# Experts of a sparse-attention + MoE kernel: the last seven token tiles computed inside a branch on a count of used tiles

## The chip, the core and the metric

The kernel runs on one core of one Trainium2 chip. The metric is the device time of one execution in microseconds; lower is better. A core has five engines that run their own instruction streams and meet only at semaphores: TensorE (PE, matrix multiplies, with its weight loads shown as PEld), VectorE (DVE), ScalarE (ACT), GpSimd (POOL) and SyncE (SP, which here only issues transfers). A name with a q behind it (POOLq, PEldq) stands for the sequencer of that engine: the part that reads instructions, waits at semaphores, loads registers and takes branches.

## The reference

Eight batches of 576 tokens go through eight heads of attention of width 64 (four heads with a local window of 32, four with a stride of 32). The result, laid out as 4608 rows of 512 numbers, goes through a mixture of experts with one expert for each token:

```python
logits = np.einsum('bsd,de->bse', x, w_gate)
local_gate = 1.0 / (1.0 + np.exp(-np.einsum('bsd,de->bse', x, w_local).squeeze(-1)))
for b in range(B):
    prev_e = -1
    for s in range(S):
        fresh_e = int(np.argmax(logits[b, s]))
        if s == 0 or local_gate[b, s] < 0.5:
            e = fresh_e
        else:
            e = prev_e if prev_e >= 0 else fresh_e
        prev_e = e
        ...
        h = np.maximum(x[b, s] @ w1[e], 0.0)
        out[b, s] = p[e] * (h @ w2[e])
```

w1 of one expert is 512 x 1024 and w2 is 1024 x 512, all in f32. So each expert takes the rows that were routed to it, and the number of rows differs from expert to expert. With the inputs of the reference (fixed seed) the eight experts get 701, 469, 606, 495, 656, 452, 546 and 683 rows.

## The kernel before

**Attention** (0 to about 190 us) writes the 4608 rows `x` to a buffer `xd` in device memory and keeps gate probabilities and expert codes on chip. **Routing** (`route`, to about 243 us) counts the rows of each expert, rounds each count up to tiles of 128 rows (`nti`, `nt`), and gives each row a slot in a list of tiles in which expert follows expert. The list has a fixed length of `NT = (4608 + 8*127)//128 = 43` tiles, which is enough for every possible routing. Routing leaves four tables: `et` (the expert of each of the 43 tiles), `gi` and `si` (for each slot the row to read and the row to write) and `ps_slot` (its probability). A slot that no token holds reads row 0 and has a row number behind the end of `out`, so its write is dropped.

**Experts** (`experts`, from about 243 us to the end) goes through the 43 tiles, numbered j = 0 to 42 here. Each tile has five steps:

- `load(j)`: SP reads the tile's expert number from `et` into a register and issues the transfers of w1 and w2 of that expert, 2 MB each, into one of four buffers (`wp`, bufs=4); POOL gathers the 128 rows of `xd` into `xg` (`xp`, bufs=3) with an indirect transfer.
- `turn_x(j)`: four PE transposes into `xps`, then DVE copies them to `xgT`.
- `hidden(j)`: 2 x 4 x 4 products of 128x128 with w1 (64 PE rows in the profile, since an f32 product is done in two passes); ACT does the two ReLUs.
- `output(j)`: eight products of 128x512 with w2 (16 rows); ACT scales the result by `ps_slot` into `y`.
- at the end of `output(j)` POOL scatters `y` to `out` with an indirect transfer.

The program is written with a framework that traces these Python loops, orders the instructions of each engine by a scheduler of its own and puts in all semaphore waits. A buffer is reused only when its last reader has signalled: the gather of `xg` for tile j+3 waits until PE has transposed tile j, and the transfers of w1 and w2 for tile j+4 wait until PE has done `hidden(j)` and `output(j)`. Each engine works through its own list strictly in order.

Around all this stands one branch that exists already: `passes` is run once, then a count `bad` is loaded into a register of every engine (L98), and a second, careful pass is run only when it is above zero (L100). It is not run with these inputs. On the way that is not taken, each engine adjusts the semaphores that the skipped instructions would have raised; on POOL this is an instruction named INC_SWDGE_SEM, which adds to the eight semaphores of POOL's transfers.

Of the kernel before, what the change touches and what calls it, by code (L numbers as in the profile page):

```python
# [8 lines left out]
F32 = mybir.dt.float32  # L9
BF16 = mybir.dt.bfloat16  # L10
I32 = mybir.dt.int32
Act = mybir.ActivationFunctionType
Alu = mybir.AluOpType
# [5 lines left out]
P = 128  # L19
B, H, S, DH = 8, 8, 576, 64  # L20
D = H * DH
E, F = 8, 1024
DK, FK = D // P, F // P
N = B * S
# [16 lines left out]


NT = (N + E * (P - 1)) // P
SKIP = 8192
NEG = -8.0e9

# [36 lines left out]
@with_exitstack  # L83
def attention_then_scomoe(ctx: ExitStack, tc: tile.TileContext, q, k, vl, vs, wg, w1, w2, out):


    nc = tc.nc
    once = ctx.enter_context(tc.tile_pool(name="once", bufs=1))
    dram = ctx.enter_context(tc.tile_pool(name="dram", bufs=1, space=DRAM))
    xd = dram.tile([N, D], F32, name="xd")  # L90
    ident = once.tile([P, P], F32, name="ident")
    make_identity(nc, ident)
    sums = once.tile([P, B * PAIRS * 2, 2, 3], F32, name="sums")
    nc.gpsimd.memset(sums, 1.0)
    bad = once.tile([1, 1], I32, name="bad")

    passes(tc, False, q, k, vl, vs, wg, w1, w2, out, xd, ident, sums, bad)
    again = nc.values_load(bad[0:1, 0:1], min_val=0, max_val=P,  # L98
                           skip_runtime_bounds_check_because="a count of partitions")
    with tc.If(again > 0):  # L100
        passes(tc, True, q, k, vl, vs, wg, w1, w2, out, xd, ident, sums, bad)


def passes(tc, careful, q, k, vl, vs, wg, w1, w2, out, xd, ident, sums, bad):
    with ExitStack() as ctx:
        slots = ctx.enter_context(tc.tile_pool(name="slots", bufs=1))
        gi = slots.tile([P, NT], I32, name="gi")
        si = slots.tile([P, NT], I32, name="si")
        ps_slot = slots.tile([P, NT], F32, name="ps_slot")
        et = slots.tile([1, NT], I32, name="et")  # L110
        with ExitStack() as first:
            routing = first.enter_context(tc.tile_pool(name="routing", bufs=1))
            probs = routing.tile([LQ, LT, B, E], F32, name="probs")
            codes = routing.tile([LQ, LT, B, E], F32, name="codes")
            with ExitStack() as part:
                attention(part, tc, careful, q, k, vl, vs, wg, xd, ident, probs, codes, sums)
            with ExitStack() as part:
                route(part, tc, ident, probs, codes, gi, si, ps_slot, et)
            if not careful:
                with ExitStack() as part:  # L120
                    bounds(part, tc, sums, bad)
        with ExitStack() as part:
            experts(part, tc, xd, w1, w2, out, ident, gi, si, ps_slot, et)


def bounds(ctx, tc, sums, bad):

    nc = tc.nc
    bp = ctx.enter_context(tc.tile_pool(name="bp", bufs=1))
    bps = ctx.enter_context(tc.tile_pool(name="bps", bufs=1, space=PSUM))  # L130
    flat = sums.rearrange("p u h i -> p (u h i)")
    ok = bp.tile([P, B * PAIRS * 12], F32, name="ok")
    nc.vector.tensor_scalar(ok, flat, SUM_LO, None, Alu.is_ge)
    nc.vector.scalar_tensor_tensor(ok, flat, SUM_HI, ok, Alu.is_le, Alu.mult)
    low = bp.tile([P, 1], F32, name="low")
    nc.vector.tensor_reduce(low, ok, axis=AX.X, op=Alu.min)
    one = bp.tile([P, 1], F32, name="one")
    nc.vector.memset(one, 1.0)
    ps = bps.tile([1, 1], F32, name="bps")
    nc.tensor.matmul(ps, lhsT=low, rhs=one, start=True, stop=True)  # L140
    nc.vector.tensor_scalar(bad, ps, -1.0, float(P), Alu.mult, Alu.add)
# [254 lines left out]
def route(ctx, tc, ident, probs, codes, gi, si, ps_slot, et):  # L396

    nc = tc.nc
    rp = ctx.enter_context(tc.tile_pool(name="rp", bufs=1))
    pp = ctx.enter_context(tc.tile_pool(name="rps", bufs=1, space=PSUM))  # L400
# [32 lines left out]
    ones = rp.tile([R, S], F32, name="ones")  # L433
# [6 lines left out]
    for t in range(LT):  # L440
        nc.tensor.matmul(cps[:, t // 3, (t % 3) * LQ:(t % 3 + 1) * LQ],
                         lhsT=codes[:, t].rearrange("p b e -> p (b e)"), rhs=ident[0:LQ, 0:LQ],
                         start=True, stop=True)
# [21 lines left out]
    nt = rp.tile([R, 1], F32, name="nt")  # L465
# [5 lines left out]
    nc.vector.tensor_tensor(end, nn[0:E, 2:3], nt[0:E], op=Alu.add)  # L471
    over = rp.tile([E, NT], F32, name="over")
    nc.vector.tensor_scalar(over, io[0:E, 0:NT], end, None, Alu.is_ge)
    eps = pp.tile([1, NT], F32, name="eps")
    nc.tensor.matmul(eps, lhsT=ones[0:E, 0:1], rhs=over, start=True, stop=True)
    nc.vector.tensor_scalar(et, eps, float(E - 1), None, Alu.min)
    base = rp.tile([R, 1], F32, name="base")
    nc.vector.tensor_scalar(base, nn[:, 2:3], float(P), nn[:, 1:2], Alu.mult, Alu.add)
    nc.vector.tensor_scalar(base, base, -1.0, None, Alu.add)
# [37 lines left out]
    skip = rp.tile([P, NT], F32, name="skip")  # L517
    nc.vector.tensor_scalar(skip, tab[:, 0], 0.0, float(SKIP), Alu.is_equal, Alu.mult)
    nc.vector.tensor_tensor(row, row, skip, op=Alu.add)
# [3 lines left out]
def experts(ctx, tc, xd, w1, w2, out, ident, gi, si, ps_slot, et):  # L523


    nc = tc.nc
    wp = ctx.enter_context(tc.tile_pool(name="wp", bufs=4))
    xp = ctx.enter_context(tc.tile_pool(name="xp", bufs=3))
    psx = ctx.enter_context(tc.tile_pool(name="psx", bufs=2, space=PSUM))
    psh = ctx.enter_context(tc.tile_pool(name="psh", bufs=4, space=PSUM))  # L530
    psy = ctx.enter_context(tc.tile_pool(name="psy", bufs=2, space=PSUM))
    T = [dict() for _ in range(NT)]
    HB = 4

    def load(j):
        t = T[j]
        e = nc.values_load(et[0:1, j:j + 1], engines=[ET.SP], min_val=0, max_val=E - 1,
                           skip_runtime_bounds_check_because="a count of at most 8 experts, held to 7")
        t["w1"] = wp.tile([P, DK, F], F32, name="w1t")
        nc.sync.dma_start(out=t["w1"], in_=w1[bass.ds(e, 1)].rearrange("o (k p) f -> p (o k) f", p=P))  # L540
        t["w2"] = wp.tile([P, FK, D], F32, name="w2t")
        nc.sync.dma_start(out=t["w2"], in_=w2[bass.ds(e, 1)].rearrange("o (k p) f -> p (o k) f", p=P))
        t["x"] = xp.tile([P, D], F32, name="xg")
        nc.gpsimd.indirect_dma_start(out=t["x"], out_offset=None, in_=xd,  # L544
                                     in_offset=bass.IndirectOffsetOnAxis(ap=gi[:, j:j + 1], axis=0))

    def turn_x(j):
        t = T[j]
        ps = psx.tile([P, D], F32, name="xps")
        for kk in range(DK):  # L550
            nc.tensor.transpose(ps[:, kk * P:(kk + 1) * P], t["x"][:, kk * P:(kk + 1) * P], ident)  # L551
        t["xT"] = xp.tile([P, D], F32, name="xgT")
        nc.vector.tensor_copy(t["xT"], ps)  # L553

    def hidden(j):
        t = T[j]
        t["hT"] = xp.tile([P, FK, P], F32, name="hT", bufs=2)
        for g in range(FK // HB):
            ps = psh.tile([P, HB, P], F32, name="hps")
            for i in range(HB):  # L560
                c = slice((g * HB + i) * P, (g * HB + i + 1) * P)
                for kk in range(DK):
                    nc.tensor.matmul(ps[:, i], lhsT=t["w1"][:, kk, c], rhs=t["xT"][:, kk * P:(kk + 1) * P],  # L563
                                     start=(kk == 0), stop=(kk == DK - 1))
            nc.scalar.activation(t["hT"][:, g * HB:(g + 1) * HB], ps, Act.Relu)  # L565

    def output(j):
        t = T[j]
        ps = psy.tile([P, D], F32, name="yps")
        for kk in range(FK):  # L570
            nc.tensor.matmul(ps, lhsT=t["hT"][:, kk], rhs=t["w2"][:, kk, :],  # L571
                             start=(kk == 0), stop=(kk == FK - 1))
        y = xp.tile([P, D], F32, name="y")
        nc.scalar.activation(y, ps, Act.Copy, scale=ps_slot[:, j:j + 1])  # L574
        nc.gpsimd.indirect_dma_start(out=out, out_offset=bass.IndirectOffsetOnAxis(ap=si[:, j:j + 1], axis=0),  # L575
                                     in_=y, in_offset=None, bounds_check=N - 1, oob_is_err=False)

    load(0)
    load(1)
    turn_x(0)  # L580
    for j in range(NT):
        if j + 2 < NT:
            load(j + 2)
        hidden(j)
        if j + 1 < NT:
            turn_x(j + 1)
        output(j)


def _strided(a):  # L590
# [45 lines left out]
```

## Time and profile before

| what | us |
|---|---|
| median of 3 runs (lowest to highest) | 891.71 (890.55 to 892.64) |
| the profiled execution: time | 892.51 |
| the profiled execution: span from first to last instruction | 890.8 |
| PE busy in the span | 830.6 (93%) |
| DVE, ACT, POOL busy | 170.2, 159.9, 93.3 |
| mean granted TensorE clock | 0.958 |

The span is what the trace covers; 1.7 us of the profiled execution's time lie outside it. Busy time counts real work of an engine and leaves out the sequencers' waits, register loads and branches. "PEclk" in a table of stages is the share of full TensorE speed that was granted there. All times in the text are counted from the start of the span.

### The profile page before, as it was taken

How to read it: one execution, taken by the hardware profiler on the slowest of the kernel's cores; microseconds unless marked ns; L12 is line 12 of the kernel's file. 1: busy time of each engine (PE TensorE's matmuls, PEld its weight loads, DVE VectorE, ACT ScalarE, POOL GpSimd, SP SyncE). 2: the span in 40 equal slices, each digit the busy share in tenths (PEclk: the TensorE clock that was granted, in tenths of full speed). 3: DMA queues.
4: the chain of work that ended last, by engine and by line, in shares of the span. 5: the costliest groups of instructions: out<-in, count | busy, mean ns of one | idle time of the engine just before them, and what ended most of it. 6: DMA issues, size and time to landing. Idle time of an engine off the chain costs nothing. (4 is left out here: it accounts for less than half of the span.)

```text
span 890.8 us, 13129 instructions
## 1 busy us (share of the span) xinstructions
PE 830.6 (93%) x5562; PEld 633.5 (71%) x5562; DVE 170.2 (19%) x469; ACT 159.9 (18%) x259; POOL 93.3 (10%) x108
## 2 busy tenths in 40 slices
PE   6999999954779999999999999999999999999993
PEld 6877777843757676868677777767686767777671
DVE  4656666668110000000000000000000000000000
ACT  2444444420001111111111111111111111111110
POOL 1000000002120011111111111111111111111000
PEclk9999999985569999999999999999999999999997
DMA  9676666110099999999898999999989989899100
GB/s 359 228 233 224 230 226 229 54 53 1 25 398 398 401 400 399 400 390 315 324 327 324 332 319 340 316 343 315 335 308 327 321 327 323 319 338 318 68 2 3
DMA packets 91411, 242.63 MB, mean 272 GB/s; under 512 B 4878, under 2 KB 14094, under 8 KB 91344
## 3 DMA queue, kind: packets, MB, share of 16 engines
q1 hardware_dynamic: 83936, 220.92, 69.3%
q0 software_dynamic: 6880, 20.72, 6.0%
q8 instruction: 46, 0.75, 0.3%
q14 instruction: 21, 0.17, 0.1%
q10 hardware_dynamic: 528, 0.07, 0.0%
HBM read 222.81 MB, written 20.71 MB: 273 GB/s over the span
## 5 line engine op out<-in xcount | busy, mean ns | idle before, releaser
L563 PEld LDWEIGHTS hps<-xgT,w1t 128*128 128x128 f32 x2752 | 315.8, 193 | 20.1 <-issue 20.1
L563 PE MATMUL hps<-xgT,w1t 128*128 128x128 f32 x2752 | 315.9, 276 | 0.0
L571 PE MATMUL yps<-w2t,hT 128*128 128x512 f32 x688 | 302.4, 592 | 0.0
L571 PEld LDWEIGHTS yps<-w2t,hT 128*128 128x128 f32 x688 | 127.4, 190 | 144.0 <-issue 144.0
L553 DVE COPY xgT<-xps 128x512 f32<-128x512 f32 x43 | 29.7, 691 | 584.1 <-PE xps L551 558.8
L565 ACT ACTIVATE hT<-hps 128x512 f32<-128x512 f32 x86 | 51.3, 597 | 270.6 <-PE hps L563 270.6
L574 ACT ACTIVATE y<-yps,ps_slot 128x512 f32<-128x512 f32 x43 | 29.5, 687 | 286.3 <-PE yps L571 286.3
L575 POOL DMA_INDIRECT out_dram<-y,si x43 | 43.0, 1001 | 339.0 <-ACT y L574 339.0
L240 PE MATMUL sps<-qt,kt 64*128 64x96 f32 (+2 forms) x704 | 63.6, 295 | 6.8 <-DMA kt<-in_k_dram 6.8
L544 POOL DMA_INDIRECT xg<-xd,gi x43 | 42.4, 986 | 237.9 <-PE xps L551 207.3
L240 PEld LDWEIGHTS sps<-qt,kt 64*128 64x128 f32 (+2 forms) x704 | 48.0, 189 | 20.0 <-issue 11.6
L244 ACT ACTIVATE e<-sps 128x576 f32<-128x576 f32 (+1 forms) x64 | 41.9, 655 | 46.9 <-PE sps L240 33.5
L286 PE MATMUL tps<-vlt,e 128*96 128x96 f32 x384 | 41.1, 258 | 0.8
L286 PE MATMUL tps<-vst,e 108*108 108x108 f32 (+1 forms) x320 | 40.2, 273 | 0.7
L286 PEld LDWEIGHTS tps<-vlt,e 128*96 128x96 f32 x384 | 36.0, 168 | 4.1 <-ACT xT L322 2.3
L286 PEld LDWEIGHTS tps<-vst,e 108*108 108x108 f32 (+1 forms) x320 | 34.6, 180 | 4.4 <-ACT xT L322 2.2
L551 PE MATMUL xps<-ident,xg 128*128 128x128 f32 x172 | 28.3, 291 | 7.8 <-DMA xg<-xd,gi 7.8
L247 DVE TENSOR_TENSOR e<-e,maskL 128x576 f32<-128x576 f32 x32 | 24.3, 758 | 36.7 <-ACT e L244 36.7
L512 PE MATMUL tab<-put,lane 96*128 96x86 f32 x96 | 20.7, 422 | 11.1 <-DVE put L504 11.1
L512 PEld LDWEIGHTS tab<-put,lane 96*128 96x128 f32 x96 | 20.6, 332 | 11.2 <-issue 11.2
L551 PEld LDWEIGHTS xps<-ident,xg 128*128 128x128 f32 x172 | 21.5, 151 | 9.4 <-issue 7.9
L247 DVE TENSOR_TENSOR e<-e,maskS 108x648 f32<-108x648 f32 (+1 forms) x32 | 24.2, 756 | 16.9 <-ACT e L244 16.9
(130 smaller groups left out, 246.7 us busy)
## 6 DMA issues: line engine op xcount, KB each, us to landing
w1t<-in_w_dram SPq DMA_DIRECT2D x43, 2048.0 KB
w2t<-in_w_dram SPq DMA_DIRECT2D x43, 2048.0 KB
kt<-in_k_dram SPq DMA_DIRECT2D x16, 608.0 KB
qt<-in_q_dram SPq DMA_DIRECT2D x16, 576.0 KB
vlt<-in_vl_dram SPq DMA_DIRECT2D x8, 780.0 KB
vst<-in_vs_dram SPq DMA_DIRECT2D x8, 650.0 KB
xd<-xl SPq DMA_DIRECT2D x8, 576.0 KB
xd<-xs SPq DMA_DIRECT2D x24, 108.0 KB
```

The source lines that it names most:

```text
L240: nc.tensor.matmul(ps[0:kb, h, i * w:(i + 1) * w], lhsT=kt[r, u.i2, c:c + kb], rhs=qt[r, u.i2, c:c + w], start=True, stop=True)
L244: nc.scalar.activation(ev, ps[0:kb, :, 0:m * w], Act.Exp, bias=0.0, scale=1.0 / DH ** 0.5)
L247: nc.vector.tensor_tensor(blocks(ev, m), blocks(ev, m), mask, op=Alu.mult)
L286: nc.tensor.matmul(ps[0:w, h, o:o + w], lhsT=u.e[0:kb, h, i * w:(i + 1) * w], rhs=vt[0:kb, u.i2, u.t0 + i, c:c + w], start=True, stop=True)
L512: nc.tensor.matmul(tab, lhsT=lane[:, i], rhs=put[:, i], start=(i == 0), stop=(i == CM - 1))
L544: nc.gpsimd.indirect_dma_start(out=t["x"], out_offset=None, in_=xd, in_offset=bass.IndirectOffsetOnAxis(ap=gi[:, j:j + 1], axis=0))
L551: nc.tensor.transpose(ps[:, kk * P:(kk + 1) * P], t["x"][:, kk * P:(kk + 1) * P], ident)
L553: nc.vector.tensor_copy(t["xT"], ps)
L563: nc.tensor.matmul(ps[:, i], lhsT=t["w1"][:, kk, c], rhs=t["xT"][:, kk * P:(kk + 1) * P], start=(kk == 0), stop=(kk == DK - 1))
L565: nc.scalar.activation(t["hT"][:, g * HB:(g + 1) * HB], ps, Act.Relu)
L571: nc.tensor.matmul(ps, lhsT=t["hT"][:, kk], rhs=t["w2"][:, kk, :], start=(kk == 0), stop=(kk == FK - 1))
L575: nc.gpsimd.indirect_dma_start(out=out, out_offset=bass.IndirectOffsetOnAxis(ap=si[:, j:j + 1], axis=0), in_=y, in_offset=None, bounds_che ...
```

## The change

Routing writes one more number: the sum over the experts of their tile counts, that is, how many of the 43 tiles hold at least one token. It is put behind the 43 entries of `et`. The smallest value it can have is 4608/128 = 36 (`NT_MIN`). In `experts`, tiles 0 to 35 stay as they were. Ahead of tile 36 all five engines load the count into a register (`used`). For tiles 36 to 42, `hidden(j)` and `output(j)` (with the scatter of `y`) stand in a branch that is taken only where `used > j`; the loads of w1, w2 and `xg` and the transposes stay outside of the branch and are done for all 43 tiles. In these seven tiles `turn_x(j+1)` stands ahead of `hidden(j)`, no longer between `hidden(j)` and `output(j)`.

```diff
+NT_MIN = N // P
...
-        et = slots.tile([1, NT], I32, name="et")
+        et = slots.tile([1, NT + 1], I32, name="et")
...
-    eps = pp.tile([1, NT], F32, name="eps")
-    nc.tensor.matmul(eps, lhsT=ones[0:E, 0:1], rhs=over, start=True, stop=True)
-    nc.vector.tensor_scalar(et, eps, float(E - 1), None, Alu.min)
+    eps = pp.tile([1, NT + 1], F32, name="eps")
+    nc.tensor.matmul(eps[:, 0:NT], lhsT=ones[0:E, 0:1], rhs=over, start=True, stop=True)
+    nc.tensor.matmul(eps[:, NT:], lhsT=ones[0:E, 0:1], rhs=nt[0:E], start=True, stop=True)
+    nc.vector.tensor_scalar(et[:, 0:NT], eps[:, 0:NT], float(E - 1), None, Alu.min)
+    nc.vector.tensor_copy(et[:, NT:], eps[:, NT:])
...
     for j in range(NT):
+        if j == NT_MIN:
+            used = nc.values_load(et[0:1, NT:NT + 1], min_val=NT_MIN, max_val=NT,
+                                  skip_runtime_bounds_check_because="the sum of the experts' tiles")
         if j + 2 < NT:
             load(j + 2)
-        hidden(j)
-        if j + 1 < NT:
-            turn_x(j + 1)
-        output(j)
+        if j < NT_MIN:
+            hidden(j)
+            if j + 1 < NT:
+                turn_x(j + 1)
+            output(j)
+        else:
+            if j + 1 < NT:
+                turn_x(j + 1)
+            with tc.If(used > j):
+                hidden(j)
+                output(j)
```

The scheduler treats each branch as one piece and orders the rest around it, so the instruction lists move more than the diff shows.

PE, end of the experts, before. The names are `hps` (hidden), `xps` (transposes), `yps` (output); the last rows are tiles 39 to 42 (four groups of hidden and output, the transposes between them belong to tiles 40, 41 and 42):

```order
L563 MATMUL hps<-xgT,w1t 128x128 x32
L551 MATMUL xps<-ident,xg 128x128 x4
L571 MATMUL yps<-w2t,hT 128x512 x8
L563 MATMUL hps<-xgT,w1t 128x128 x32
L551 MATMUL xps<-ident,xg 128x128 x4
L571 MATMUL yps<-w2t,hT 128x512 x8
L563 MATMUL hps<-xgT,w1t 128x128 x32
L551 MATMUL xps<-ident,xg 128x128 x4
L571 MATMUL yps<-w2t,hT 128x512 x8
L563 MATMUL hps<-xgT,w1t 128x128 x32
L571 MATMUL yps<-w2t,hT 128x512 x8
```

PE, the same place with the change, from `hidden(35)` to the start of tile 38's branch:

```order
L566 MATMUL hps<-xgT,w1t 128x128 x32
L554 MATMUL xps<-ident,xg 128x128 x4
L574 MATMUL yps<-w2t,hT 128x512 x8
L554 MATMUL xps<-ident,xg 128x128 x16
L586 TENSOR_LOAD et
L598 COMPARE_AND_BRANCH
L566 MATMUL hps<-xgT,w1t 128x128 x32
L574 MATMUL yps<-w2t,hT 128x512 x8
L598 UNCONDITIONAL_BRANCH x2
L598 COMPARE_AND_BRANCH
L566 MATMUL hps<-xgT,w1t 128x128 x32
L574 MATMUL yps<-w2t,hT 128x512 x8
```

After `output(35)` PE now does sixteen transposes in a row, those of tiles 37, 38, 39 and 40, before it loads `used` and starts tile 36. (Of the two unconditional branches in a row, the first ends the taken way, the second the way that skips the tile.) The transposes of tiles 41 and 42 stand together behind tile 38's branch.

POOL, from the gather of tile 39 to the third branch, with the change:

```order
L547 DMA xg<-xd,gi 128x512 x2
L578 DMA out_dram<-y,si 4608x512
L547 DMA xg<-xd,gi 128x512 x2
L586 TENSOR_LOAD et
L598 COMPARE_AND_BRANCH
L578 DMA out_dram<-y,si 4608x512
L598 UNCONDITIONAL_BRANCH
L598 ISA
L598 UNCONDITIONAL_BRANCH
L598 COMPARE_AND_BRANCH
L578 DMA out_dram<-y,si 4608x512
```

The four gathers are those of tiles 39 and 40, then 41 and 42, all ahead of the first branch; in between is the scatter of tile 35. The row "ISA" is the way that skips a tile: one INC_SWDGE_SEM for each skipped tile. Before the change POOL's list alternated gather and scatter and ended in five scatters, with no such instruction between them.

## The prediction

> **What bounds the kernel now.** I read the page's busy times and groups first, then the PE timeline of the last eight tiles, the tables of stages there, and last the sequencer rows of the end.
>
> ```profile
> PE 830.6 (93%) x5562; PEld 633.5 (71%) x5562; DVE 170.2 (19%) x469; ACT 159.9 (18%) x259; POOL 93.3 (10%) x108
> L563 PE MATMUL hps<-xgT,w1t 128*128 128x128 f32 x2752 | 315.9, 276 | 0.0
> L571 PE MATMUL yps<-w2t,hT 128*128 128x512 f32 x688 | 302.4, 592 | 0.0
> ```
>
> PE is busy 93% of the span, and 618 us of it are the two products of the experts, with no idle time before them. The PE timeline (start, length) shows the rhythm; tile 36 begins at 775.69:
>
> ```profile
> 775.69 7.31 PE L563 MATMUL hps<-xgT,w1t 128*128 128x128 f32 x64
> 782.83 0.60 PE L551 MATMUL xps<-ident,xg 128*128 128x128 f32 x4
> 783.27 7.03 PE L571 MATMUL yps<-w2t,hT 128*128 128x512 f32 x16
> 790.14 7.31 PE L563 MATMUL hps<-xgT,w1t 128*128 128x128 f32 x64
> ...
> 826.62 7.03 PE L571 MATMUL yps<-w2t,hT 128*128 128x512 f32 x16
> 833.49 7.31 PE L563 MATMUL hps<-xgT,w1t 128*128 128x128 f32 x64
> ...
> 862.39 7.31 PE L563 MATMUL hps<-xgT,w1t 128*128 128x128 f32 x64
> 869.53 7.03 PE L571 MATMUL yps<-w2t,hT 128*128 128x512 f32 x16
> ```
>
> A tile takes 790.14 - 775.69 = 14.45 us, of which 783.27 - 782.83 = 0.44 is the transposes, so 14.01 hidden and output. Tile 40 begins at 833.49, tile 42 ends at 869.53 + 7.03 = 876.56. Tables of stages for tiles 36 to 39, for tiles 40 to 42, and for one tile's length late in the program (columns: window, its length, busy PE, PEld, DVE, ACT, POOL, PE clock, DMA share, GB/s):
>
> ```profile
> 775.69:833.49 57.80, 57.80 (x338) 42.50 (x336) 2.76 (x4) 7.53 (x12) 6.98 (x7) 1.00 0.82 290
> 833.49:876.60 43.11, 43.08 (x249) 31.25 (x247) 1.38 (x2) 5.64 (x9) 2.99 (x3) 1.00 0.02 4
> 848.00:862.00 14.00, 14.00 (x85) 10.41 (x84) 0.69 (x1) 1.88 (x3) 0.99 (x1) 1.00 0.01 2
> ```
>
> PE is never idle there, DMA is at 0.82 and then nearly empty: PE alone sets the time. A scatter of 128 full rows would be 256 KB, 18 GB/s over 14 us; the last window shows 2, so that tile writes nothing. That fits the counts of the reference: 701, 469, 606, 495, 656, 452, 546 and 683 rows make 6+4+5+4+6+4+5+6 = 40 tiles. Tiles 40, 41 and 42 are empty and will be skipped.
>
> **The change part by part.** *Three tiles leave the path.* PE's last product moves from the end of tile 42 (876.56) to that of tile 39, 826.62 + 7.03 = 833.65: **-42.9 us**.
>
> *Their weights are still loaded.* SP's last transfer, w2 of tile 42, and DMA around it:
>
> ```profile
> 819.23 0.37 SPq L542 DMA_DIRECT2D w2t<-in_w_dram  x1
> 820.00:828.00 8.00, 8.00 (x65) 7.28 (x65) 0.69 (x1) 1.19 (x2) 1.00 (x1) 1.00 0.87 306
> 828.00:834.00 6.00, 6.00 (x19) 2.89 (x18) 0.00 (x0) 0.31 (x1) 0.00 (x0) 1.00 0.00 1
> ```
>
> It is issued when tile 38 frees its buffer (819.04) and is over by about 828, nine us later. With the change it still hangs on tile 38, so it ends some five us before tile 39 does: hidden by PE, **0**. Were that cover gone it would be at most 9 us.
>
> *The gathers of tiles 38 to 40 become a wait of PE.* The order shows PE doing the transposes of tiles 37 to 40 between `output(35)` and tile 36. `xg` has three buffers, so the gather of tile 40 cannot start until tile 37 is transposed, which PE does just before, at 775.69. The gathers on POOL, and the time from issue to landing of those near here:
>
> ```profile
> 783.71 0.99 POOL L544 DMA_INDIRECT xg<-xd,gi  x1 [5.85 <-PE xps L551]
> DMA to landing us min/median/max: 6.9/7.6/8.4
> ```
>
> A gather starts 783.71 - 782.83 = 0.88 after the transposes that free its buffer. So tile 40's starts at 775.69 + 0.88 = 776.57 and lands 7.6 later, at 784.2 (783.5 to 785.0), among the same weight traffic as before. Behind that wait on PE stand tile 40's transposes, the load of `used` and all of tile 36; the copies of DVE and the scatter on POOL wait behind it without delaying anyone. Transposes and register load take about 1.1 us side by side (1.09 in the next fence, 0.49 for the load in the one after). Tile 36 starts at 785.3 instead of 775.69: **+9.6**.
>
> *PE's clock.* PE has no product from about 778 (tile 39's gather lands about then, its transposes follow) to 784.2, six us. What idling does to the clock, and what a restart costs:
>
> ```profile
> 876.60:880.30 3.70, 0.00 (x0) 0.00 (x0) 0.00 (x0) 0.69 (x1) 0.98 (x1) 1.00 0.02 5
> 880.40:890.80 10.40, 0.00 (x0) 0.00 (x0) 0.00 (x0) 0.00 (x0) 0.00 (x0) 0.50 0.00 1
> 254.64 1.09 PE L551 MATMUL xps<-ident,xg 128*128 128x128 f32 x4 [1.27 <-DMA xg<-xd,gi]
> 255.52 9.03 PE L563 MATMUL hps<-xgT,w1t 128*128 128x128 f32 x64
> ```
>
> 3.7 us after the last product the clock falls to 0.50, and the first hidden stage after such a stretch took 9.03 instead of 7.31. I take **+1.7**; below it is 0, if short transposes keep the clock up, above 3.4, if the half clock lasts twice as long.
>
> *Transposes.* Of the four groups that stood in tiles 36 to 39, those of tiles 37 to 40 are now ahead of tile 36 (in the 9.6) and two remain, behind tile 38: -4 x 0.44 + 2 x 0.44 = **-0.9**. PE's last product then ends at 833.65 + 9.6 + 1.7 - 0.9 = **844.1**.
>
> *Branches of tiles 36 to 39.* The rows of the branch that exists already, with the loads before it and what follows it, and POOL's scatter:
>
> ```profile
> L98 PEldq TENSOR_LOAD <-bad x1: 487/487/487, 870.4 to 870.4; - x1
> L100 PEldq COMPARE_BRANCH  x1: 3462/3462/3462, 871.0 to 871.0; - x1
> L100 PEldq EVENT_SEMAPHORE  x1: 51/51/51, 876.6 to 876.6; - x1
> L98 POOLq TENSOR_LOAD <-bad x1: 511/511/511, 877.3 to 877.3; - x1
> 877.56 0.98 POOL L575 DMA_INDIRECT out_dram<-y,si  x1 [13.03 <-ACT y L574]
> L100 POOLq COMPARE_BRANCH  x1: 53/53/53, 877.9 to 877.9; - x1
> L100 POOLq EVENT_SEMAPHORE  x5: 17/43/43, 880.5 to 880.8; - x5
> L100 POOLq INC_SWDGE_SEM  x1: 1908/1908/1908, 880.9 to 880.9; - x1
> L632 POOLq DRAIN  x3: 40/107/7088, 882.9 to 890.5; - x3
> DMA to landing us min/median/max: 2.1/2.5/2.6
> L628 POOLq INC_SWDGE_SEM  x1: 27/27/27, 0.2 to 0.2; - x1
> ```
>
> PE's sequencer loaded `bad` at 870.4, six us before its array was done (876.56), and had its whole branch of 3.46 us behind it by 874.5. The same lead covers the conditional tiles, which fall through their compare: **0**, and up to 4 x 3.46 = 13.8 without it. ACT needs its second branch only 3 us after `y`; hidden.
>
> *The end.* Before, 890.80 - 876.56 = 14.2 us follow the last product. They run through POOL: scatter, branch (877.9 to 880.5, 2.6 us until the next instruction), INC_SWDGE_SEM 1.9, then a DRAIN of 7.1; the scatter lands after 2.5 and sets nothing. With the change, three skips stand between scatter and branch. Each has one INC_SWDGE_SEM on POOL: 3 x 1.9 = 5.7. Their six branches at 0.05 are 0.3; the first INC_SWDGE_SEM waits for the end of the scatter's issue (878.5) where the branch went ahead at 877.9, 0.6; the load of `bad` (0.5) is no longer under the scatter. **+7.1**, together 21.3. From below one INC_SWDGE_SEM costs 0.03 (the row at the program's start, in another use); from above 1.9 + 7.1 = 9.0, if the DRAIN is its own aftermath. I take 1.9, the row with the same use. PE and ACT pass their skips under this: even four fetches of 3.46 on PE end some six us before POOL.
>
> *Routing.* One more product and one more cast of a single number:
>
> ```profile
> 205.27 2.08 PE L488 MATMUL slps<-inb,slot 64*96 64x8 f32 x12 [0.61 <-DVE slot L481]
> 207.39 0.20 DVE L496 CAST sli<-slps 96x48 int32<-96x48 f32 x1 [2.07 <-PE slps L488]
> ```
>
> They fit into 0.61 us of idle PE and 2.07 of idle DVE: **0**, and without them 0.4.
>
> *Sum.* 844.1 + 21.3 = span 865.4, against 890.8: -25.4. The profiled execution was 892.51; its time lies 0.8 above the median 891.71. I take the difference from the median: **866.3 us**.
>
> **Rivals.**
>
> *B, the end is cheaper.* INC_SWDGE_SEM at 0.03 gives 866.3 - 5.6 = 860.7, without the clock's fall 859. Equally, if the first of them does early what the DRAIN does late, 866.3 - 7.1 = 859. For it: the 27 ns row. Against: the row with 1.9 is the same addition.
>
> *C, each taken branch costs a fetch of code.* On POOL 2.6 us passed after the compare, so six taken branches cost 15.6 instead of 0.3: 881.6. Against: that branch jumps over the whole careful pass, the skips over a dozen POOL instructions. [...]
>
> *F, PE does not run ahead through the branches.* Four conditional tiles at 3.46: 880.1. Against: the 870.4 row.
>
> *D, each INC_SWDGE_SEM brings its DRAIN.* 3 x 7.1 = 21.3 more: 887.6. For it: nothing else in the rows tells what the DRAIN waits for, since the scatter had landed by 880.1.
>
> *E, slower.* A skip costs POOL both: 1.9 + 7.1 + 2 x 2.6 = 14.2, three of them 42.6 where I put 6.0: 866.3 + 36.6 = 902.9. It turns slower once a skip costs 10.5 us, that is 25.4/3 over my 2.0.
>
> *The count comes out as 43, nothing is skipped.* Then only the wait remains: 891.7 + 9.6 + 1.7 - 0.9 = 902. The empty scatter speaks against it.
>
> **How the numbers follow.** Forecast 0.56 (own range 861 to 871: landing, clock, half an INC_SWDGE_SEM), B 0.14, C 0.10, F 0.08, D 0.07, E and the count of 43 0.05. About 0.2% is what a measurement of this kernel tells from no change, 1.8 us. All but the last case lie below that: faster 0.94, within 0.01, slower 0.05. From 857 to 882 leaves out D, E and slivers of B and C, 0.18.
>
> **What would show it.** In the changed profile: no L566/L574 products after about 844, three tiles fewer; a PE idle of about 6 us before tile 36's hidden stage, ended by the gather of `xg`; the PE clock at 0.50 for some us there and a first hidden stage near 9.0; conditional tiles of 14.0 each; three INC_SWDGE_SEM on line L598 of POOL of 1.9 each and one DRAIN of 7.1; weights landing before tile 39's end. I am wrong if PE waits for weights or ACT in tiles 36 to 39, if the wait ahead of tile 36 is missing, or if more than 25 us follow the last product.

## The result, and the profile after

| | before | changed |
|---|---|---|
| median of 4 runs, us (lowest to highest) | 892.17 (890.55 to 893.35) | 867.43 (865.65 to 868.38) |
| profiled execution: time, span | 892.51, 890.8 | 866.83, 865.1 |
| last product ends | 876.56 | 842.97 |
| from there to the end of the span | 14.2 | 22.1 |

The changed kernel takes 0.9722 of the time before (95% interval 0.9698 to 0.9745), 24.7 us less. The prediction said 866.3. PE lost three tiles: its line of busy times in the profile's page has 238 rows fewer than before, and 38 us less work.

```profile
PE 792.3 (92%) x5324; PEld 605.3 (70%) x5324; DVE 170.2 (20%) x470; ACT 154.1 (18%) x250; POOL 90.1 (10%) x105
```

The PE timeline of the changed kernel from the output of tile 35 on (start, length, engine, line, work; in brackets the idle time before it and what ended it):

```profile
768.04 7.03 PE L574 MATMUL yps<-w2t,hT 128*128 128x512 f32 x16
774.91 1.04 PE L554 MATMUL xps<-ident,xg 128*128 128x128 f32 x8
776.29 0.66 PE L554 MATMUL xps<-ident,xg 128*128 128x128 f32 x4 [0.35 <-issue]
783.79 1.09 PE L554 MATMUL xps<-ident,xg 128*128 128x128 f32 x4 [6.84 <-DMA xg<-xd,gi]
784.67 8.52 PE L566 MATMUL hps<-xgT,w1t 128*128 128x128 f32 x64
...
827.92 1.04 PE L554 MATMUL xps<-ident,xg 128*128 128x128 f32 x8
...
835.94 7.03 PE L574 MATMUL yps<-w2t,hT 128*128 128x512 f32 x16
```

Three groups of transposes (tiles 37 to 39) run at once, the fourth (tile 40) comes 6.84 us later, when its gather has landed. Tile 36's hidden stage starts 784.67 - 774.91 = 9.76 us after tile 35's last product and takes 8.52 instead of 7.31. From then on PE does not wait; the transposes of tiles 41 and 42 stand behind tile 38 (827.92) and take 0.87, and the last product ends at 835.94 + 7.03 = 842.97. The gather behind the wait (POOL's timeline, then the time from issue to landing of the gathers from 770 to 800):

```profile
775.78 0.96 POOL L547 DMA_INDIRECT xg<-xd,gi  x1 [6.32 <-PE xps L554]
DMA to landing us min/median/max: 7.5/7.7/7.9
```

It was issued 775.78 - 774.91 = 0.87 after the transposes of tiles 37 and 38 began, and took 7.9, the longest of the three, until just before PE's transposes at 783.79. In the table of stages (window, length, busy PE, PEld, DVE, ACT, POOL, then the PE clock, DMA share, GB/s) the clock falls in the idle stretch and is not full again at once:

```profile
778.00:784.00 6.00, 0.21 (x1) 0.24 (x2) 0.00 (x0) 0.00 (x0) 1.98 (x3) 0.69 0.99 333
785.00:800.00 15.00, 15.00 (x81) 11.17 (x81) 0.69 (x1) 1.19 (x2) 0.00 (x0) 0.93 0.48 160
```

The end, from POOL's scatter of tile 39 on: its row of the timeline, and the sequencer rows of the three skipped branches (L598), of the branch around the careful pass (L101) and of the program's end (L645). Such a row gives shortest, median and longest length in ns, and the first and last start in us:

```profile
844.02 0.98 POOL L578 DMA_INDIRECT out_dram<-y,si  x1 [13.95 <-ACTq L598]
L598 PEldq COMPARE_BRANCH  x11: 73/174/421, 784.4 to 843.6; - x11
L598 POOLq COMPARE_BRANCH  x11: 34/39/50, 777.8 to 848.0; - x11
L598 POOLq INC_SWDGE_SEM  x3: 1795/1800/1837, 844.1 to 848.2; - x3
L101 POOLq COMPARE_BRANCH  x1: 45/45/45, 850.4 to 850.4; - x1
L101 POOLq EVENT_SEMAPHORE  x6: 17/30/43, 853.2 to 853.7; - x6
L101 POOLq INC_SWDGE_SEM  x1: 1828/1828/1828, 855.6 to 855.6; - x1
L645 POOLq DRAIN  x3: 46/107/6842, 857.4 to 864.8; - x3
```

POOL runs through three INC_SWDGE_SEM of 1.8 from 844.1 on, reaches the far branch at 850.4 (7.4 after the last product; before it was 1.3), has its next instruction 2.8 later, stands 1.9 between the sixth EVENT_SEMAPHORE (853.7) and the INC_SWDGE_SEM (855.6), where before there was 0.1, and drains for 6.84. The sum is 22.1.

All runs in one table. "Last product" is where PE's last row ends, "end" what follows it. Ratios are to the kernel before, on the same chip.

| run | us | ratio (95%) | last product | end |
|---|---|---|---|---|
| changed kernel | 867.43 | 0.972 (0.970 to 0.975) | 843.0 | 22.1 |
| e1_xg8: eight buffers | 860.32 | 0.965 (0.963 to 0.967) | 837.8 | 20.2 |
| e2_inside: transposes inside | 855.44 | 0.959 (0.957 to 0.961) | 834.0 | 20.5 |
| e4_always: nothing skipped | 903.38 | 1.012 (1.010 to 1.015) | 885.5 | 16.2 |
| e6_static40: no branch | 848.35 | 0.951 (0.949 to 0.953) | 834.3 | 13.6 |
| e10_pad: code moved by 8 | 865.33 | 0.970 (0.968 to 0.972) | 842.8 | 20.1 |
| e7_more: 43 more gathers | 875.92 | 0.982 (0.980 to 0.984) | 846.2 | 27.9 |
| e9_drain: early drains | 852.59 | 0.955 (0.953 to 0.957) | 842.1 | 8.8 |
| e14_drain36: one early drain | 855.74 (one run) | | 843.8 | 10.2 |
| e15_beforedrain: before, one drain | 884.53 | 0.993 (0.991 to 0.994) | 874.5 | 6.7 |
| e8_nest3: inside, nested | 851.88 | 0.954 (0.953 to 0.956) | 834.6 | 16.8 |
| e13_drain_xg8: two edits | 851.01 | 0.953 (0.951 to 0.955) | 839.5 | 10.9 |
| e12_nest3drain: all of it | 842.06 | 0.944 (0.942 to 0.945) | 833.0 | 7.4 |

### The profile page after: what moved, and what is told of

Its sections match the earlier page's. It is cut to its first block, busy times and chain, and to the rows that moved or that the text cites. A ratio compares the mean times of both kernels' runs of the same rounds, so it can differ in the third digit from the quotient of the medians.

```text
span 865.1 us, 12699 instructions
## 1 busy us (share of the span) xinstructions
PE 792.3 (92%) x5324; PEld 605.3 (70%) x5324; DVE 170.2 (20%) x470; ACT 154.1 (18%) x250; POOL 90.1 (10%) x105
## 3 DMA queue, kind: packets, MB, share of 16 engines
q0 software_dynamic: 6640, 20.72, 6.3%
## 4 chain that ended last, share of the span: by engine, by line
issue 41%; PE 31%; DMA 15%; POOL 4%; ACT 3%; DVE 3%; POOLq 0%; SPq 0%; ACTq 0%
DMA out_dram<-y,si 13%; PE tps L287 9%; PE hps L566 5%; PE yps L574 5%; PE sps L241 4%; POOL out_dram L578 2%; PE tab L515 2%; POOL xg L547 2%; PE tps L340 2%; PE tps L329 1%; ACT xT L332 1%; ACT xT L323 1%; DMA xg<-xd,gi 1%; PE tps L346 1%; PE tps L321 1%
## 5 line engine op out<-in xcount | busy, mean ns | idle before, releaser
L566 PEld LDWEIGHTS hps<-xgT,w1t 128*128 128x128 f32 x2560 | 294.8, 193 | 17.8 <-issue 17.7
L566 PE MATMUL hps<-xgT,w1t 128*128 128x128 f32 x2560 | 295.0, 276 | 0.0
L574 PE MATMUL yps<-w2t,hT 128*128 128x512 f32 x640 | 281.3, 592 | 0.0
L574 PEld LDWEIGHTS yps<-w2t,hT 128*128 128x128 f32 x640 | 118.5, 190 | 133.9 <-issue 133.9
L568 ACT ACTIVATE hT<-hps 128x512 f32<-128x512 f32 x80 | 47.8, 597 | 263.5 <-PE hps L566 263.5
L577 ACT ACTIVATE y<-yps,ps_slot 128x512 f32<-128x512 f32 x40 | 27.5, 687 | 264.9 <-PE yps L574 258.6
L578 POOL DMA_INDIRECT out_dram<-y,si x40 | 40.0, 1000 | 319.8 <-ACT y L577 305.5
L547 POOL DMA_INDIRECT xg<-xd,gi x43 | 42.3, 983 | 226.2 <-PE xps L554 200.9
L248 DVE TENSOR_TENSOR e<-e,maskS 108x648 f32<-108x648 f32 (+1 forms) x32 | 24.2, 757 | 16.8 <-ACT e L245 16.8
```

The costliest lines, as they stand in the source:

```text
L248: nc.vector.tensor_tensor(blocks(ev, m), blocks(ev, m), mask, op=Alu.mult)
```

## The experiments

### Is it the gather that holds PE?

**Eight buffers for xg.**

```diff
-        t["x"] = xp.tile([P, D], F32, name="xg")
+        t["x"] = xp.tile([P, D], F32, name="xg", bufs=8)
```

> The changed kernel with eight buffers for xg instead of three, so that the gathers of tiles 38 to 40 need not wait for PE's transposes. Theory (the gather of tile 40 holds PE ahead of tile 36, and the clock falls in that idle): the 6.84 us of idle PE and the 8.52 - 7.31 = 1.21 us of slow hidden stage both go, 867.4 - 8.1 = 859.4 us, and tile 36's hidden stage begins some 2.5 us after tile 35's last product (four groups of transposes and the register load). Rival (PE is held by the load of the count or by the branch's own start, not by the gather): about 867 us, idle PE of some 6 us as before.

860.32 us. The PE timeline of this kernel, at the start of the experts and ahead of tile 36:

```profile
264.86 8.80 PE L574 MATMUL yps<-w2t,hT 128*128 128x512 f32 x16 [3.24 <-DMA w2t<-in_w_dram]
...
771.07 7.03 PE L574 MATMUL yps<-w2t,hT 128*128 128x512 f32 x16
777.94 1.04 PE L554 MATMUL xps<-ident,xg 128*128 128x128 f32 x8
779.32 1.25 PE L554 MATMUL xps<-ident,xg 128*128 128x128 f32 x8 [0.35 <-DVE xgT L556]
780.66 7.40 PE L566 MATMUL hps<-xgT,w1t 128*128 128x128 f32 x64
```

No transpose waits for a gather, and tile 36 starts 2.7 us after tile 35 instead of 9.76, at a full clock: 7.0 and 1.1 us gone, as the theory said. The total came near its 859.4 only because two things that it did not contain cancel in part. At the start of the experts PE now waits 3.24 us for w2 of tile 0, and tile 35's output starts 3.0 later (771.07 against 768.04). With eight buffers POOL issues its first eight gathers without a wait between 240.1 and 250.0, while the first weights are being loaded, where the changed kernel issues five; that these hold up w2 is likely, but no run shows it alone. And the end is 1.9 shorter, without the standstill ahead of the last INC_SWDGE_SEM.

**Transposes inside the branch.**

```diff
-            if j + 1 < NT:
-                turn_x(j + 1)
             with tc.If(used > j):
                 hidden(j)
+                if j + 1 < NT:
+                    turn_x(j + 1)
                 output(j)
```

> The changed kernel with the transposes of tile j+1 inside the branch of tile j, between hidden and output, as the kernel before has them. Theory: the whole 9.76 us ahead of tile 36 and the 1.21 us of slow clock go, the two groups of transposes behind tile 38 (0.87) go, four groups inside tiles 36 to 39 come back (4 x 0.44 = 1.76): 867.4 - 9.76 - 1.21 - 0.87 + 1.76 = 857.4 us, and the end after the last product stays at about 22. Rival (PE passes the branches for nothing only because the transposes stood ahead of them; with waits inside the blocks each costs its fetch of 3.46): 4 x 3.46 more, 871 us.

855.44 us. The PE timeline of this kernel from the output of tile 35 to tile 37:

```profile
769.16 7.03 PE L574 MATMUL yps<-w2t,hT 128*128 128x512 f32 x16
776.03 7.31 PE L566 MATMUL hps<-xgT,w1t 128*128 128x128 f32 x64
...
790.48 7.31 PE L566 MATMUL hps<-xgT,w1t 128*128 128x128 f32 x64
```

Tile 36 follows tile 35 without a gap, and a tile is back at 790.48 - 776.03 = 14.45. The whole wait came from where the transposes stood: outside the branches, the scheduler had put four groups ahead of the first of them, with three buffers to hold their rows. The rival of 871 us falls: entering a branch costs PE nothing that can be seen here. Of the 2.0 us under the 857.4 expected, 1.6 is the shorter end: the standstill ahead of the last INC_SWDGE_SEM is missing here too.

### What do the branches themselves cost?

**Nothing skipped.**

```diff
-            with tc.If(used > j):
+            with tc.If(used > 20):
```

(and 0 as the lower bound given for the count, so that the comparison stays)

> The changed kernel with the condition used > 20 in all seven branches, so that they are all entered and nothing is skipped: all 43 tiles are computed. Theory (the price of the branches is the wait ahead of tile 36 and nothing else; the longer end comes from skipping): three tiles of 14.0 more than the changed kernel up to the last product, 842.97 + 42.0 = 885.0, and the end of the kernel before, 14.2: span 899.2, time 900.9 us. Rival (the end is longer because the branches are there, taken or not): end of 22.1, time 908.8 us. Second rival (POOL has to fetch its far code a second time whatever was skipped): end of 16.1, time 902.8 us.

903.38 us, 1.2% slower than before. The last product ends at 878.43 + 7.03 = 885.46, and 16.2 follow:

```profile
L101 POOLq COMPARE_BRANCH  x1: 50/50/50, 886.8 to 886.8; - x1
L101 POOLq EVENT_SEMAPHORE  x6: 17/30/43, 889.4 to 889.9; - x6
L101 POOLq INC_SWDGE_SEM  x1: 1908/1908/1908, 891.8 to 891.8; - x1
L645 POOLq DRAIN  x3: 46/107/7087, 893.7 to 901.4; - x3
```

POOL is at the far branch 1.3 us after the last product, as before the change. So the 6.1 us by which it is later in the changed kernel belong to the three skips, and the first rival (908.8) falls. The standstill of 1.9 between sixth EVENT_SEMAPHORE and INC_SWDGE_SEM is here too although nothing was skipped. So the theory's end of 14.2 is missed, and the second rival (end of 16.1, 902.8 us) came nearest. This run shares its code with the changed kernel but for one constant.

**No branch at all.** A loop over 40 tiles.

```diff
-    for j in range(NT):
-        if j == NT_MIN:
+    NU = 40
+    for j in range(NU):
+        if False:
...
-        if j < NT_MIN:
+        if True:
```

(the loads and transposes go up to tile 39; the count is computed, but not loaded, and there is no branch on it)

> The kernel without any branch or count in the loop over tiles, with a fixed 40 tiles in place of 43; tiles 40 to 42 (empty with these inputs) are left out altogether, so it is right for these inputs alone. It gives the bound that the branches could reach. Theory: three tiles of 14.45 and nothing else, 892.2 - 43.35 = 848.8 us, end after the last product 14.2, or 13.7 if the last DRAIN on POOL takes 82 ns for each of POOL's transfers (80 instead of 86 of them: 6.59 us instead of 7.09), 848.3 us. Rival (the empty tiles were shorter or were partly hidden): 855 us or more.

848.35 us, 848.3 expected; DRAIN 6.598, 6.59 expected, and an end of 13.6:

```profile
L646 POOLq DRAIN  x3: 40/107/6598, 840.4 to 847.6; - x3
```

The last product ends 42.3 us earlier than before (834.3), and the time is 43.3 under that of the kernel before in the same comparison; the changed kernel got 24.7 of this. The empty tiles' weights, which it loads and this one does not, cost it nothing: in both profiles none of PE's waits in the experts is ended by a transfer of weights.

**Eight more instructions on POOL at the start.**

```diff
+    pad = once.tile([1, 8], F32, name="pad")
+    for i in range(8):
+        nc.gpsimd.memset(pad[:, i:i + 1], 0.0)
     passes(tc, False, q, ...)
```

> The changed kernel with eight more small memsets on POOL at the program's start, which move all code of POOL behind them by eight instructions. Theory (the 1.9 us between the last EVENT_SEMAPHORE and the INC_SWDGE_SEM after the far branch are a second code fetch, because the code lies across the edge of a fetched piece there): the gap falls to about 0.1, 867.4 - 1.9 = 865.5 us. Rival (the gap comes from the branches ahead of it): it stays, 867.4 us.

865.33 us. The same rows as above, with the far branch two lines further down in the code:

```profile
L104 POOLq COMPARE_BRANCH  x1: 45/45/45, 850.3 to 850.3; - x1
L104 POOLq EVENT_SEMAPHORE  x6: 17/30/43, 852.9 to 853.3; - x6
L104 POOLq INC_SWDGE_SEM  x1: 1832/1832/1832, 853.4 to 853.4; - x1
```

Sixth EVENT_SEMAPHORE and INC_SWDGE_SEM stand 0.1 apart, where the changed kernel has 1.9. Only the position of POOL's code differs. The transfers show the same: the queue of instruction fetches from the far branch to the start of DRAIN, first of the changed kernel, then of this one (packets, MB, share):

```profile
q14 instruction: 3, 0.02, 1.2%
```

```profile
q14 instruction: 2, 0.02, 1.2%
```

The changed kernel's second packet starts at 853.85, 0.13 after the sixth EVENT_SEMAPHORE has ended, and the INC_SWDGE_SEM starts 1.7 after that, as the first instruction behind the far branch starts 1.6 after the first packet (851.65); here the second packet (853.49) falls under the INC_SWDGE_SEM and holds up nothing. So I read the standstill as a wait for a second fetch: with the code moved by eight instructions it went, as the theory of an edge between fetched pieces expected, though no view shows the edge itself. The skips' branches, 0.03 to 0.05 us on POOL, have no standstill like these: in the changed kernel the three INC_SWDGE_SEM of 1.8 and the branches between them run from 844.1 to 850.0. The far branch has 2.8 us until the next instruction there and 2.6 here, and the standstill behind it cost another 1.9.

### What do DRAIN and INC_SWDGE_SEM pay for?

Three profiles so far gave a DRAIN of 7.088, 6.842 and 6.598 us with 86, 83 and 80 transfers issued by POOL (gathers and scatters): 82.4 ns for each, every time.

**43 more gathers.**

```diff
         nc.gpsimd.indirect_dma_start(out=t["x"], out_offset=None, in_=xd,
                                      in_offset=bass.IndirectOffsetOnAxis(ap=gi[:, j:j + 1], axis=0))
+        z = xp.tile([8, D], F32, name="z")
+        nc.gpsimd.indirect_dma_start(out=z, out_offset=None, in_=xd,
+                                     in_offset=bass.IndirectOffsetOnAxis(ap=gi[0:8, j:j + 1], axis=0))
```

> The changed kernel with one more gather behind each of the 43 gathers of xg: eight rows of xd into a small tile that nothing reads. POOL issues 126 transfers instead of 83. Theory (the last DRAIN on POOL takes about 82 ns for every transfer that POOL has issued; 7.088/86, 6.842/83 and 6.598/80 in the runs so far): DRAIN 126 x 82.4 ns = 10.4 us, time 867.4 + 3.5 = 871 us (869 if the gap of 1.9 ahead of POOL's last INC_SWDGE_SEM goes with the moved code). Rival (it goes by rows, 8 of 128 each): DRAIN 7.1 us, 867.7 us. Second rival (it has nothing to do with the transfers): DRAIN 6.8, 867.4 us.

875.92 us, above all three. The skips and the program's end:

```profile
L601 POOLq INC_SWDGE_SEM  x3: 2666/2667/2697, 847.3 to 853.1; - x3
L648 POOLq DRAIN  x3: 46/107/10352, 862.9 to 873.8; - x3
```

The DRAIN is the theory's (10.4 expected), so it goes by transfers and not by rows. It doesn't go by packets either: the profile's page counts 8016 packets for POOL's queue against 6640, a fifth more, where the DRAIN is half as long again. What nobody expected is that INC_SWDGE_SEM grew too, from 1.80 to 2.67, and with the one behind the far branch there are four of them: 3.5 us. Another 3.2 were lost up to the last product (846.2 against 843.0), at the start of the experts: with the added gathers between those of `xg`, the first hidden stage begins at 258.96, 4.0 later than in the changed kernel. The standstill of 1.9 is gone.

**A drain of POOL in each conditional tile.**

```diff
             with tc.If(used > j):
+                nc.gpsimd.drain()
                 hidden(j)
```

> The changed kernel with a drain of POOL as the first instruction of every conditional tile; it runs in tiles 36 to 39, while POOL waits for y anyway. Theory (a DRAIN pays 82 ns for each transfer since the last one): the first takes some 6.5 us under PE's products, the next ones 0.2 or less, and the one at the end some 0.3 instead of 6.84: 867.4 - 6.5 = 860.9 us, or 859.0 if the gap of 1.9 ahead of POOL's last INC_SWDGE_SEM goes with the moved code. Rival (a DRAIN has a price of its own or counts all transfers since the start): every one takes about 7 us, 867.4 us or 865.5.

852.59 us, 6.4 under the lower of the expected values. The rows of the end, and last those of the four early DRAINs:

```profile
L598 POOLq INC_SWDGE_SEM  x3: 155/160/193, 843.2 to 844.0; - x3
L101 POOLq COMPARE_BRANCH  x1: 45/45/45, 844.6 to 844.6; - x1
L101 POOLq EVENT_SEMAPHORE  x6: 17/30/43, 848.6 to 849.0; - x6
L101 POOLq INC_SWDGE_SEM  x1: 193/193/193, 849.1 to 849.1; - x1
L646 POOLq DRAIN  x3: 46/107/125, 849.3 to 850.6; - x3
...
L599 POOLq DRAIN  x4: 7566/8098/12918, 777.2 to 828.2; - x4
```

The DRAIN at the end fell from 6.84 to 0.125, and each INC_SWDGE_SEM from 1.80 to 0.16 (the last from 1.83 to 0.19): four times 1.64 is the 6.6 that the theory lacked. The standstill is gone here, but the far branch takes 4.0 us until the next instruction (844.6 to 848.6); why it is longer than the 2.8 of the changed kernel, the runs don't show. The early DRAINs (last row) were not short. Those of tiles 37 to 39 have one transfer on the list each (one issued since the last DRAIN) and took 7.6 to 8.4: each ended 0.1 after the scatter issued just before had landed (7.5 to 8.3 us from issue to landing there). The first, in tile 36, took 12.9: with 79 transfers on the list it ended 3.3 after the last gather had landed (786.88); 6.5 in all had been expected. POOL has that time: its next work is the next `y`, 14 us later.

**One drain, in tile 36.**

```diff
             with tc.If(used > j):
+                if j == NT_MIN:
+                    nc.gpsimd.drain()
                 hidden(j)
```

> The changed kernel with one drain of POOL, in tile 36 alone. At the end the list then holds the scatters of tiles 36 to 39, four transfers. Theory (a straight line through the runs so far): DRAIN 0.125 + 3 x 0.082 = 0.37 us, INC_SWDGE_SEM 0.16 + 3 x 0.0215 = 0.22 us each, time about 853.1 us. Rival (a DRAIN near the end is what counts, since an older one's effect is lost): DRAIN and INC_SWDGE_SEM well above that.

```profile
L598 POOLq INC_SWDGE_SEM  x3: 215/220/258, 844.9 to 845.8; - x3
L647 POOLq DRAIN  x3: 46/107/382, 852.5 to 853.7; - x3
```

Four transfers: 0.382 and 0.22, as expected (0.37 and 0.22). The time, 855.7 in a single run, lies 2.6 above its 853.1; the profile has the standstill of 1.9 behind the far branch again, this time between the fourth and the fifth EVENT_SEMAPHORE. Over 1, 4, 80, 83, 86 and 126 transfers a straight line gives 0.05 + 0.082 n us for the DRAIN at the end; over 1, 4, 83 and 126 about 0.13 + 0.020 n for the INC_SWDGE_SEM of a skip.

**The kernel before, with one drain.**

```diff
-        output(j)
+        if j == NT - 4:
+            flag = nc.values_load(et[0:1, j:j + 1], min_val=0, max_val=2 * E, ...)
+            with tc.If(flag < E):
+                nc.gpsimd.drain()
+                output(j)
+        else:
+            output(j)
```

> The kernel before (43 tiles, no count) with one drain of POOL ahead of the scatter of tile 39; to hold it at its place, the output of tile 39 stands in a branch that is always entered. Theory (DRAIN and INC_SWDGE_SEM at the end go by the transfers since the last DRAIN, with or without the change): four scatters are left, DRAIN 0.38 instead of 7.09, INC_SWDGE_SEM 0.25 instead of 1.91: 892.3 - 8.4 = 883.9 us, up to 1.9 more if the moved code of POOL gets the second fetch. Rival (the early DRAIN holds up POOL where somebody waits): about 892 us, DRAIN at the end small all the same.

884.53 us, 0.9925 of before (0.9908 to 0.9942), 6.8 us less, with a DRAIN of 382 ns at the end (L639) where there were 7088. The list has nothing to do with the change; the change only met it three times more.

```profile
L100 POOLq INC_SWDGE_SEM  x1: 268/268/268, 878.9 to 878.9; - x1
L639 POOLq DRAIN  x3: 46/107/382, 879.2 to 880.9; - x3
```

### Put together

**Transposes inside, the last three branches nested**, so that one branch skips them all (loads stay outside).

```diff
+    def tail(j, n):
+        with tc.If(used > j):
+            hidden(j)
+            if j + 1 < NT:
+                turn_x(j + 1)
+            output(j)
+            if n > 1:
+                tail(j + 1, n - 1)
...
+        elif j < NT - 3:
+            tail(j, 1)
+        elif j == NT - 3:
+            tail(j, 3)
```

> Transposes inside the branches, between hidden and output, and the branches of tiles 40, 41 and 42 nested, so that a count of 40 skips all three by one branch. Theory (each skipped block that holds a transfer of POOL costs one INC_SWDGE_SEM, 2.0 us with what stands around it; in the run with the transposes inside alone the time was 855.4): two of them go, 855.4 - 4.0 = 851.4 us. Rival (the skip of three nested blocks adjusts as much as three skips): 855.4 us.

851.88 us, with one INC_SWDGE_SEM for the three tiles (1.86, against 1.80 for one tile): here a skip of three tiles pays once.

**Early drains and eight buffers on the changed kernel** (the two short edits shown above).

> The changed kernel with two short edits: eight buffers for xg, and a drain of POOL as the first instruction of every conditional tile. Theory (the wait of PE and POOL's long list are independent of each other): 852.6 - 7.1 (what the buffers alone brought up to the last product and at the clock) = 845.5 us. Rival (the first drain waits for the gathers in flight, and with more of them in flight it reaches into the scatter of tile 36): 848 us or more.

851.01 us, a miss: the buffers add almost nothing to the drains. The wait is gone here too, but so is the gain. The PE timeline of this kernel at the start of the experts and at tile 35, then that row of the version with drains alone:

```profile
266.48 8.80 PE L574 MATMUL yps<-w2t,hT 128*128 128x512 f32 x16 [3.03 <-DMA w2t<-in_w_dram]
...
772.69 7.03 PE L574 MATMUL yps<-w2t,hT 128*128 128x512 f32 x16
```

```profile
767.40 7.03 PE L574 MATMUL yps<-w2t,hT 128*128 128x512 f32 x16
```

The wait for w2 at the start is back (3.03, and the output behind it takes 8.80 instead of 7.03), and tile 35 is 772.69 - 767.40 = 5.3 us late. All of that is there already at tile 1, whose hidden stage begins at 275.12 against 269.83. Another 2.3 goes to the standstill behind the far branch, which this code has. So of the 8 us that the wait for the gather and its clock cost, little is left: 0.5 by the spans (850.9 and 850.4), 1.6 by the medians. The rival's price (848 or more) came true, its reason did not: the first DRAIN took 10.5 us, ended at 791.7, and the scatter of tile 36 came at 797.6.

**Nested, with drains.**

```diff
         with tc.If(used > j):
+            nc.gpsimd.drain()
             hidden(j)
```

(this edit is against the version before, with the nested branches)

> The version with transposes inside the branches and the last three branches nested (851.9 us), and with a drain of POOL as the first instruction of every conditional tile. Theory (what DRAIN and INC_SWDGE_SEM take goes by the transfers that POOL has issued since its last DRAIN): the DRAIN at the end falls from 6.84 to 0.2 or less, both INC_SWDGE_SEM from 1.85 to 0.2: 851.9 - 6.7 - 3.3 = 841.9 us, one more if the far branch again takes 4 us instead of 2.7 as in the run with drains. Rival (the drains hold up POOL's gathers, which are issued between the blocks here, and PE waits for them): 845 to 850 us.

842.06 us, 0.9435 of before (0.9417 to 0.9453): below the version with 40 fixed tiles, though it serves every count. That version has no early drain, though. With one it would, by the rows here, save 6.5 us of DRAIN and 1.6 of INC_SWDGE_SEM, so an estimate for it is 840.3 us (not run), and the branches then cost about 2 us. The rows of the end, and a table of stages:

```profile
L585 POOLq INC_SWDGE_SEM  x1: 214/214/214, 834.2 to 834.2; - x1
L652 POOLq DRAIN  x3: 46/107/128, 838.8 to 840.1; - x3
775.00:833.00 58.00, 57.95 (x337) 42.30 (x335) 2.77 (x4) 7.53 (x12) 6.94 (x7) 1.00 0.83 290
```

PE is busy for 57.95 of 58 us over the last four tiles (last row, table of stages), and 7.4 us follow its last product; 3.1 of them are the far branch of POOL (834.9 to 838.0).

## Why the prediction was right, and where it was not

- **Three tiles, -42.9.** Right: without branches the last product ends 42.3 earlier and the time is 43.3 shorter, 0.5 of it by the shorter DRAIN.
- **Weights of the empty tiles, 0.** Right: PE never waits for them. The last transfer is issued at 828.12 and DMA is nearly empty from 837 on (0.03), six us before tile 39 ends.
- **The wait for the gather, +9.6.** 9.76, with the idle PE ended by the gather of `xg` as said. Eight buffers, or the transposes inside, take it away.
- **The clock, +1.7.** 1.2, from 8.52 - 7.31. The granted clock was 0.50 for 6.8 us, from 780.3 to 787.2, in the changed kernel. What the hidden stage lost is half of what of these 6.8 us falls into it: 787.2 - 784.7 = 2.5, half of it 1.2. In the five others with the wait the same stage took 8.22 to 8.81, so it lost 0.9 to 1.5. The row that the prediction took, 9.03, stands behind a slow stretch of 65 us at 0.50 (194 to 259), 3.6 us of which reach into it, so its 1.7 was the share of another stage and came near by luck. From the first transposes after the wait (783.79) to the full clock it is 3.4 us in the changed kernel; for the five others an estimate, twice the time that the hidden stage lost counted from its start, gives 2.7 to 3.9.
- **Transposes, -0.9.** Right: 0.87 behind tile 38, none in the other tiles. PE was through with tile 35 at 774.91, 0.8 earlier than in the profile before; the difference is there already at tile 1's hidden stage (270.47 against 271.25), and its cause was not followed. With these, 844.1 became 842.97.
- **Branches of tiles 36 to 39, 0.** Right; tiles of 14.0 in a row, and rivals F and C fall with them: a near branch costs 0.03 to 0.05 us on POOL, and up to 0.42 on PE's sequencer, where the far one took 3.46 before.
- **The end, +7.1.** Mis-sized: it was +7.9, and that is so close only because errors cancel. Up to the far branch I had put 7.1 and it was 6.1: the first INC_SWDGE_SEM starts at 844.1, it does not wait for the scatter's issue (0.6), and they are 1.8. The DRAIN was 0.25 shorter. Against that stand 1.9 for a second code fetch, which the prediction had nowhere, and 0.2 more for the first (2.8 instead of 2.6). Over the whole span errors cancel once more: 865.1 against 865.4, with the last product 1.1 earlier than forecast and the end 0.8 longer.
- **What INC_SWDGE_SEM and DRAIN are.** The values were taken from rows of the same use, which was the right choice for the sum, but the reason was wrong. The 1908 ns row is long because of the transfers that POOL had issued, not because of its use: the INC_SWDGE_SEM of a skip, 1.80 in the changed kernel, takes 0.16 once a drain stands ahead of it. The 27 ns row at the program's start, which rival B rested on, stands ahead of all transfers; that the straight line gives 0.13 for none shows that the number of transfers is not all of the difference. Rival B's price could have been had; what the changed kernel lacked was the drain.
- **Rival D** took the DRAIN for an aftermath of INC_SWDGE_SEM. It comes once, and pays for the list. **The count of 43** falls with the three skips.

## What to carry to other kernels

Before work is put into a branch, look where the instructions that stay outside of it will go: a scheduler that treats a branch as one piece collects them ahead of it, and buffers sized for the old rhythm turn that into a wait (here 11 us of the 19 by which the changed kernel missed the gain of 40 fixed tiles). Price a skipped branch at what its adjustments cost on the engine that ends last, and put branches that fall together into one. Where an engine's end is a long DRAIN, try an early one at a place where that engine waits anyway; here it brought 7 us on the kernel before and 15 on the changed one, 13 of them in the DRAIN and the four adjustments.

## What was not expected of the hardware

- DRAIN and INC_SWDGE_SEM on POOL take longer the more transfers POOL has issued since its last DRAIN: 0.082 us for each at the program's end and 0.020 in a skip, from 1 to 126 of them; the 43 gathers of eight rows counted like the others. What is kept for each transfer the traces don't show.
- A DRAIN of POOL in mid-program ended only after the landing of what was just issued. In the run with early drains it ended 0.1 us after that with one transfer on the list, and 3.3 after it with 79; over the runs with early drains it took 7.6 to 12.9 us.
- The same seven instructions of POOL behind the far branch started within 0.5 to 0.6 us of each other, or, with the standstill, within 2.4 to 2.8. Eight more instructions at the program's start, which only move the code, took the standstill of 1.9 away, so two versions can differ by 1.9 us, 0.2% of this kernel, for no reason of their own. The far branch itself took 2.6 to 4.0 us until the first of them, and what makes that spread the runs don't show.
- In the changed kernel the clock fell to 0.50 3.4 us after the last product ahead of the wait (776.95 to 780.3) and stayed there for 6.8 us, the last 3.4 of them with PE back at work.
